# A fused retention and MoE kernel on one core: paired attention blocks and DMA transposes from unit 8 on, in place of unit-by-unit heads and TensorE transposes up to unit 11

## The chip, the cores and the metric

The kernel runs on 1 core of one Trainium2 chip. The metric is the device time of one execution in microseconds (us); lower is better. All comparisons below use runs that the harness calls fast. The kernel before has two close levels, most runs at 313.1 to 313.9 us with a granted TensorE clock of 0.997 to 1.0, and some at 314.5 to 316.1 us with 0.989 to 0.995; both count as fast, so a difference under about 1% needs many runs here.

Engines are named as in the profile: PE is TensorE (PEld its weight loads), DVE VectorE, ACT ScalarE, POOL GpSimd (it issues the loads), SP SyncE (it issues outputs and DMA transposes).

## The reference

```python
# q, k, v: (8 batches, 8 heads, 576, 64) float32; w_in (512, 2048), w_out (2048, 512)
scores = (q @ k^T) / sqrt(64)                       # per batch and head
ret    = scores * Dmat                              # Dmat[i,j] = gamma_h ** (i-j) for i >= j, else 0
attn   = ret @ v
x = attn.transpose(0, 2, 1, 3).reshape(4608, 512)
h = x @ w_in
out = (h * sigmoid(1.702 * h)) @ w_out              # (4608, 512)
```

## The kernel before

The 4608 rows are cut into 36 *units* of 128 rows; four units make a *chunk* of 512 rows. For each unit the attention part needs k and q with the head dimension on the partitions (`qkT`). A unit then takes: `scores` (8 small matmuls from qkT, masked by DVE into `pm`), `inter` (from the running state `kv`), `values` (from `pm` and the scaled v, `vp`), `values_out` (into `xT`), and `state` (updates kv from k and vp). `up` and `up_half` multiply a chunk by w_in, ACT applies the gelu; `down` multiplies by w_out, 16 steps per chunk, each of 4 matmuls of 512 columns. Attention work is slipped between these steps so that PE never waits.

qkT is made in one of two ways:

```python
def transpose_pe(u, bank, eng):           # 8 matmuls against the identity, then one DVE copy
    for j in range(2 * HP):
        op("pe", matmul(t[:, j, :], kq[sl][:, j // HP, ...], ident, is_transpose=True), ...)
    op("dve", tensor_copy(qkT[u % NQT], t), reads=[bank], writes=[f"qkT{u % NQT}"])

def transpose_dma(u):                     # one DMA, SBUF to SBUF, issued by SP
    op("sp", dma_start_transpose(qkT[u % NQT], kq[sl]),
       reads=[f"kq{sl}_0", f"kq{sl}_1"], writes=[f"qkT{u % NQT}"], dma=f"d_qkT{u % NQT}")
```

Before, units 0 to 11 are transposed on PE and units 12 to 35 by DMA. The order of loads on POOL, and the part of the program that the change touches (cut):

```python
for u in range(4, 8): load_kq(u); load_v(u)
for i in range(4):    load_wout(i)
for u in (8, 9):      load_kq(u); load_v(u)
# ... heads of units 0-3, chunk 0 up ...                      (units 10, 11 loaded here; then fetch(6))
play(8, lambda i: up_half(1, i, 1), {
    2: [lambda: head_in(8, "dve")],      # head_in = transpose_pe
    4: [lambda: head_mid(8)],            # head_mid = scores, scale v, mask
    6: [lambda: head_out(8)],            # head_out = inter, values, values_out, state
    7: [lambda: head_in(9, "dve")],
})
ready_t(6)                               # DMA transposes of units 12, 13
fetch(7, [f"qkT{13 % NQT}"])             # loads of 14, 15, held until unit 13's transpose has landed
play(16, lambda i: down(0, i, ("H0", "H1")), {
    1: [lambda: head_mid(9)],
    3: [lambda: head_in(10, "dve"), lambda: head_out(9)],
    # ... 10 and 11 in the same way, ready_t(7), fetch(8, held) ...
})
# from here on: block(m) handles units 2m and 2m+1 together, between down and up steps
```

`play(n, step, events)` runs step 0 to n-1 and the listed events after the numbered step.

Of the kernel before, what the change touches and what calls it, by code (L numbers as in the profile page):

```python
# [11 lines left out]
B, H, S, DH = 8, 8, 576, 64  # L12
# [3 lines left out]
NU = (B * S) // P  # L16
# [124 lines left out]
def bass_retnet_parallel__then__act_gelu_quick_kernel(  # L141
# [13 lines left out]
    with es:  # L155
# [40 lines left out]
        def load_kq(u, after=()):  # L196
            sl = u % NLD
            rows = unit_rows(u)
            for i, src in enumerate((k, q)):
                def f(e, src=src, i=i):  # L200
                    return [
                        e.dma_start(  # L202
                            kq[sl][p0 : p0 + n, i, :].rearrange("p (h d) -> p h d", d=DH),
                            src[b, :, s0 : s0 + n, :].rearrange("h p d -> p h d"),
                        )
                        for p0, n, b, s0 in rows
                    ]
                op("pool", f, reads=after, writes=[f"kq{sl}_{i}"], dma=f"d_kq{sl}_{i}", ndma=len(rows))

        def load_v(u, eng="pool"):  # L210
            sl = u % NVN
            rows = unit_rows(u)

            def f(e):
                return [
                    e.dma_start(  # L216
                        vn[sl][p0 : p0 + n, :, :],
                        v[b, :, s0 : s0 + n, :].rearrange("h p d -> p h d"),
                    )
                    for p0, n, b, s0 in rows  # L220
                ]
            op(eng, f, writes=[f"vn{sl}"], dma=f"d_vn{sl}_{eng}", ndma=len(rows))
# [147 lines left out]
        def inter(u):  # L370
            pb, kind, c = unit_info(u)
            qt = qkT[u % NQT]
            if c == 0:
                return
            bank = f"O{u % 2}"
            ob = by_pair(bank)
            for hp in range(HP):
                if kind < 2:
                    op("pe", lambda e, hp=hp: e.matmul(  # L379
                        ob[:, hp, :], kv[kind][c - 1][:, hp, :], qt[:, HP + hp, :],  # L380
                        start=(hp == 0), stop=True, skip_group_check=True),
                       reads=[f"kv{kind}_{c - 1}_0", f"kv{kind}_{c - 1}_1", f"qkT{u % NQT}"],
                       writes=[bank])
                else:
                    for b in range(2):
                        op("pe", lambda e, hp=hp, b=b: e.matmul(  # L386
                            ob[:, hp, 64 * b : 64 * b + 64], kv[b][3][:, hp, :],
                            qt[:, HP + hp, 64 * b : 64 * b + 64],
                            start=(hp == 0 and b == 0), stop=True, skip_group_check=True),
                           reads=[f"kv{b}_3_0", f"kv{b}_3_1", f"qkT{u % NQT}"], writes=[bank])  # L390
# [12 lines left out]
        def scores_out(u, hh, sb0=None):  # L403
            sb0 = 2 * (u % 2) if sb0 is None else sb0
            m = maskc if unit_info(u)[1] == 2 else mask
            bank = f"S{sb0 + hh}"
            op("dve", lambda e: e.tensor_tensor(  # L407
                pm[u % 4][hh].ap(), by_pair(bank), m[:, None, :].to_broadcast([P, HP, P]), ALU.mult),
               reads=[bank, "maskc" if m is maskc else "mask"], writes=[f"pm{u % 4}_{hh}"])

        def values(u):
            c = unit_info(u)[2]
            bank = f"O{u % 2}"
            ob = by_pair(bank)
            for hp in range(HP):
                for hh in range(2):
                    op("pe", lambda e, hp=hp, hh=hh: e.matmul(  # L417
                        ob[64 * hh : 64 * hh + 64, hp, :], vp[u % NVP][:, 2 * hp + hh, :],
                        pm[u % 4][hh][:, hp, :],
                        start=(c == 0 and hp == 0), stop=True, skip_group_check=True),  # L420
                       reads=[f"vp{u % NVP}", f"pm{u % 4}_{hh}"], writes=[bank])

        def values_out(u):
            ch, j = divmod(u, 4)
            ty = unit_info(u)[2]
            bank = f"O{u % 2}"
            op("dve", lambda e: e.tensor_tensor(  # L427
                xT[ch % 3][:, :, 128 * j : 128 * j + 128], by_pair(bank), gq[:, ty, :, :], ALU.mult),
               reads=[bank] + [f"gq{i}_{ty}" for i in range(HP)], writes=[f"xT{ch % 3}_{j}"])
# [65 lines left out]
        def head_in(u, eng, bank="S2"):  # L495
            transpose_pe(u, bank, eng)

        def head_mid(u):
            scores(u, 0)
            if u > 1:  # L500
                scale_v(u)
            scores_out(u, 0, 0)
            scores_out(u, 1, 0)

        def head_out(u, eng="dve"):
            inter(u)
            values(u)
            values_out(u)
            if u < 8:
                state_in_psum(u, "S3", eng)  # L510
            else:
                state(u, "S3")

        def fetch(m, after=()):
            for u in (2 * m, 2 * m + 1):
                if u < NU:
                    load_kq(u, after)
                    load_v(u)

        def ready_t(m):  # L520
            for u in (2 * m, 2 * m + 1):
                if u < NU:
                    transpose_dma(u)

        def ready_v(m):
            for u in (2 * m, 2 * m + 1):
                if u < NU:
                    scale_v(u)

        def block(m, done=False):  # L530

            a, b = 2 * m, 2 * m + 1
            nxt = 2 * m + 2 < NU
            if not done:
                inter(a)
                inter(b)
            if nxt:
                scores(a + 2)
                scores(b + 2)
                scores_out(a + 2, 0)  # L540
            if not done:
                values(a)
                values(b)
                values_out(a)
                values_out(b)
            if nxt:
                scores_out(a + 2, 1)
                scores_out(b + 2, 0)
                scores_out(b + 2, 1)
            fetch(m + 4)  # L550
            ready_t(m + 3)
            ready_v(m + 2)

        def states(m, i):
            u = 2 * m + (i == 4)
# [21 lines left out]
        for u in range(4, 8):  # L577
            load_kq(u)
            load_v(u)
        for i in range(4):  # L580
            load_wout(i)
        for u in (8, 9):
            load_kq(u)
            load_v(u)

        def play(n, step, events):
            for i in range(n):
                step(i)
                for f in events.get(i, ()):
                    f()  # L590
# [20 lines left out]
        warm(4)  # L611
        head_out(3, "act")
        setup_tail()
        for u in (10, 11):
            load_kq(u)
            load_v(u)
        warm(2)
        play(16, lambda f: up(0, f), {
            9: [lambda: head_in(4, "dve")],
# [3 lines left out]
            14: [lambda: head_mid(5)],  # L623
            15: [lambda: head_in(6, "dve"), lambda: head_out(5)],
        })
        fetch(6)
        head_mid(6)
        head_in(7, "dve")
        warm(1)
        play(8, lambda i: up_half(1, i, 0), {  # L630
            1: [lambda: head_out(6)],
            3: [lambda: head_mid(7)],
            5: [lambda: head_out(7)],
        })
        play(8, lambda i: up_half(1, i, 1), {
            2: [lambda: head_in(8, "dve")],
            4: [lambda: head_mid(8)],
            6: [lambda: head_out(8)],
            7: [lambda: head_in(9, "dve")],
        })  # L640
        ready_t(6)
        fetch(7, [f"qkT{13 % NQT}"])
        play(16, lambda i: down(0, i, ("H0", "H1")), {
            1: [lambda: head_mid(9)],
            3: [lambda: head_in(10, "dve"), lambda: head_out(9)],
            5: [lambda: head_mid(10)],
            7: [lambda: head_in(11, "dve"), lambda: head_out(10), lambda: ready_t(7), lambda: fetch(8, [f"qkT{15 % NQT}"])],
            9: [lambda: head_mid(11), lambda: ready_v(6)],
            11: [lambda: head_out(11)],
        })  # L650
        late = None
        for m in range(5, NU // 2 + 1):
            if m < NU // 2:
                block(m, m == 5)
            if late is not None:
                up(*late)
            c, h = divmod(m - 1, 2)
            iu = idn = 0
            for x in "UUDDUDUDUDUDDDUU" if m == 5 else "DDUDUDUDUDUDDUUU":
                if x == "D":  # L660
                    down(c - 1, 8 * h + idn, YB)
                    idn += 1
                else:
                    late = (c, 8 * h + iu)
                    if iu < 7:
                        up(*late)
                    iu += 1
                    states(m + 1, iu - 1)
# [62 lines left out]
```

## Time and profile before

| | before |
|---|---|
| time, median (range) of 6 runs taken with the change | 314.38 us (313.29 to 315.83) |
| PE busy | 303.9 us, 98% of the span |
| chain that ended last | PE 93% |
| DMA transposes | 24, median 12.4 us from issue to landing |

From the page of the kernel before: busy time of the engines; then PE and its granted clock in tenths over 40 slices of the span; then the engines' shares of the chain that ended last.

```profile
PE 303.9 (98%) x2174; PEld 156.4 (50%) x2174; DVE 134.3 (43%) x269; ACT 123.4 (40%) x222; POOL 106.5 (34%) x133
PE   8799999999999999999999999999999999999994
PEclk9999999999999999999999999999999999999999
PE 93%; POOL 3%; DMA 2%; DVE 1%; ACT 0%; issue 0%; POOLq 0%
```

PE is the bound, and it is not only "busy": the timeline shows matmuls of 512 columns starting 216 ns apart, without gaps. Busy time by 10 us stretches of the kernel before (columns: PE, PEld, DVE, ACT, POOL busy us with instruction counts, granted clock, DMA share, GB/s; packets overlap in the records, so a DMA share can be above 1):

```profile
50.00:60.00 10.00, 10.00 (x111) 7.65 (x110) 4.58 (x8) 4.58 (x8) 1.82 (x3) 1.00 1.79 175
60.00:70.00 10.00, 10.00 (x92) 5.36 (x90) 8.48 (x17) 1.19 (x2) 1.99 (x3) 1.00 1.19 173
70.00:80.00 10.00, 10.00 (x82) 5.04 (x77) 8.37 (x16) 2.39 (x4) 3.29 (x4) 1.00 1.44 185
80.00:90.00 10.00, 10.00 (x51) 4.63 (x49) 2.60 (x7) 3.38 (x6) 9.60 (x13) 1.00 1.27 132
```

A transpose on PE, in the timeline of the kernel before (start us, duration us, engine, line, what), is the second line here:

```profile
59.88 1.90 PE L469 MATMUL psH<-w_out_sb,gT 128*128 128x512 bf16 x8
61.62 0.61 PE L310 MATMUL psS<-ident,kq 128*128 128x128 bf16 x8
```

The next PE work starts 0.54 us after it (0.45 us for three of the four units). So four units cost PE 1.9 us. That is the most that removing these transposes can return directly.

A DMA transpose is another matter. The two lines are from the view of DMA issues of the kernel before, the first for the whole span (median us to landing), the second for 62 to 85 us, when fewer loads are queued:

```profile
qkT<-kq SPq DMA_TRANSPOSE x24, 12.4
qkT<-kq SPq DMA_TRANSPOSE x4, 3.7
```

The same instruction lands after 3.7 us or after 12.4 us, according to what else is queued.

### The profile page before, as it was taken

What the parts mean: (1) busy time and instruction counts of PE and PEld (TensorE: products, weight loads), DVE (VectorE), ACT (ScalarE), POOL (GpSimd) and SP (SyncE); (2) the same over time, 40 slices, a digit from 0 to 9 for tenths busy, and PEclk for the clock granted to TensorE, in tenths of its full rate; (3) what the DMA queues carried; (4) which work ended last, traced back from release to release, by engine and by line L of the source; (5) the groups of instructions that cost most, each with busy time, mean ns of one, the idle gap of its engine ahead of it and who ended that gap; (6) DMA issues with size and microseconds to landing.
All of it is one profiled execution on the core that took longest, in us unless ns stands there. A gap on an engine that the chain in (4) does not pass through costs nothing.

```text
span 311.3 us, 5152 instructions
## 1 busy us (share of the span) xinstructions
PE 303.9 (98%) x2174; PEld 156.4 (50%) x2174; DVE 134.3 (43%) x269; ACT 123.4 (40%) x222; POOL 106.5 (34%) x133
## 2 busy tenths in 40 slices
PE   8799999999999999999999999999999999999994
PEld 3444588655454545454545454545454545444442
DVE  4671884597445542546263625262627150100000
ACT  9676345201433333333333333333343434343411
POOL 9999933024699836154132323000000000000000
PEclk9999999999999999999999999999999999999999
DMA  9999999999999999999999999999910102010112
GB/s 133 184 206 187 190 200 184 175 172 165 173 120 207 139 141 167 141 147 159 116 150 113 153 91 173 113 175 110 161 67 2 68 2 67 2 67 34 36 67 67
DMA packets 114711, 39.14 MB, mean 126 GB/s; under 512 B 103808, under 2 KB 107904, under 8 KB 114688
## 3 DMA queue, kind: packets, MB, share of 16 engines
q0 software_dynamic: 82016, 22.55, 84.5%
q1 hardware_dynamic: 32672, 16.26, 35.8%
q8 instruction: 17, 0.28, 0.4%
q14 instruction: 6, 0.05, 0.1%
HBM read 36.70 MB, written 9.44 MB: 148 GB/s over the span
## 4 chain that ended last, share of the span: by engine, by line
PE 93%; POOL 3%; DMA 2%; DVE 1%; ACT 0%; issue 0%; POOLq 0%
PE psH L438 35%; PE psS L469 33%; PE psH L455 5%; PE psH L469 5%; PE psO L417 4%; PE psS L398 3%; PE psS L331 2%; PE psO L469 2%; POOL kq L202 2%; PE psO L379 2%; DMA kq<-in_q_dram 2%; PE psS L310 1%; PE psH L491 1%; PE psO L386 0%; POOL vn L216 0%; ACT kv_1 L344 0%
## 5 line engine op out<-in xcount | busy, mean ns | idle before, releaser
L438 PE MATMUL psH<-xT,w_in_sb 128*128 128x512 bf16 x512 | 127.3, 379 | 0.0
L443 ACT ACTIVATE gT<-psH 128x512 bf16<-128x512 f32 x128 | 76.5, 597 | 115.7 <-PE psH L438 115.7
L469 PE MATMUL psS<-w_out_sb,gT 128*128 128x512 bf16 x480 | 117.3, 379 | 0.0
L438 PEld LDWEIGHTS psH<-xT,w_in_sb 128*128 128x128 bf16 x512 | 47.8, 98 | 58.7 <-ACT gT L443 3.2
L469 PEld LDWEIGHTS psS<-w_out_sb,gT 128*128 128x128 bf16 x480 | 46.1, 98 | 51.7
L202 POOL DMA_DIRECT2D kq<-in_k_dram x40 | 37.4, 943 | 53.9 <-DMA qkT<-kq 22.4
L202 POOL DMA_DIRECT2D kq<-in_q_dram x40 | 36.8, 928 | 19.2 <-issue 19.0
L407 DVE TENSOR_TENSOR pm_0<-psS,mask 128x512 bf16<-128x512 f32 x32 | 22.0, 688 | 39.4 <-PE psS L398 39.3
L216 POOL DMA_DIRECT2D vn<-in_v_dram x38 | 35.6, 949 | 9.6 <-issue 5.1
L477 ACT ACTIVATE osb<-psS 128x512 f32<-128x512 f32 x30 | 17.9, 597 | 30.4 <-PE psS L469 30.4
L427 DVE TENSOR_TENSOR xT<-psO,gq 128x512 bf16<-128x512 f32 x36 | 23.6, 683 | 11.7 <-PE psO L417 11.7
L301 DVE TENSOR_TENSOR vp<-vn,vfac 128x512 bf16<-128x512 f32 x36 | 23.7, 685 | 1.3 <-DMA vn<-in_v_dram 1.1
L407 DVE TENSOR_TENSOR pm_1<-psS,mask 128x512 bf16<-128x512 f32 x32 | 21.8, 681 | 0.0
L361 DVE TENSOR_TENSOR kvf<-psS,kvf 64x256 f32<-64x256 f32 x24 | 10.1, 421 | 26.7 <-PE psS L331 26.5
L455 PE MATMUL psH<-xT,w_in_sb 128*128 128x256 bf16 x128 | 15.2, 273 | 0.0
L469 PE MATMUL psH<-w_out_sb,gT 128*128 128x512 bf16 x64 | 15.0, 380 | 0.0
L460 ACT ACTIVATE gT<-psH 128x512 bf16<-128x512 f32 x16 | 9.6, 598 | 11.5 <-PE psH L455 11.5
L455 PEld LDWEIGHTS psH<-xT,w_in_sb 128*128 128x128 bf16 x128 | 12.0, 98 | 1.9 <-issue 0.2
L417 PE MATMUL psO<-pm_0,vp 128*64 128x128 bf16 x144 | 12.9, 223 | 0.0
L359 DVE COPY kvf<-psS 64x256 f32<-64x256 f32 x12 | 5.1, 421 | 18.2 <-PE psS L331 18.1
L417 PE MATMUL psO<-pm_1,vp 128*64 128x128 bf16 x144 | 12.5, 223 | 0.3 <-DVE pm_1 L407 0.3
L317 DVE COPY qkT<-psS 128x1024 bf16<-128x1024 bf16 x9 | 6.2, 690 | 14.7 <-PE psS L310 14.6
(74 smaller groups left out, 179.9 us busy)
## 6 DMA issues: line engine op xcount, KB each, us to landing
out_dram<-osb SPq DMA_DIRECT2D x32, 256.0 KB, 5.7
vn<-in_v_dram POOLq DMA_DIRECT2D x30, 256.0 KB, 21.2
kq<-in_k_dram POOLq DMA_DIRECT2D x32, 128.0 KB, 18.6
kq<-in_q_dram POOLq DMA_DIRECT2D x32, 128.0 KB, 21.0
w_in_sb<-in_moe_w_in_dram POOLq DMA_DIRECT2D x4, 512.0 KB, 9.9
w_out_sb<-in_moe_w_out_dram POOLq DMA_DIRECT2D x4, 512.0 KB, 18.9
vn<-in_v_dram POOLq DMA_DIRECT2D x8, 128.0 KB, 25.6
out_dram<-osb SPq DMA_DIRECT2D x8, 128.0 KB, 5.7
```

The source lines that it names most:

```text
L202: e.dma_start(kq[sl][p0 : p0 + n, i, :].rearrange("p (h d) -> p h d", d=DH), src[b, :, s0 : s0 + n, :].rearrange("h p d -> p h d"),)
L216: e.dma_start(vn[sl][p0 : p0 + n, :, :], v[b, :, s0 : s0 + n, :].rearrange("h p d -> p h d"),)
L301: op("dve", lambda e: e.tensor_tensor(vp[u % NVP].ap(), vn[sl].ap(), vfac[:, ty, :, None].to_broadcast([P, H, DH]), ALU.mult), reads=[f"vn ...
L361: op("dve", lambda e, d=acc, s=src: e.tensor_tensor(d, s, d, ALU.add), reads=[bank, kfk], writes=[kfk])
L407: op("dve", lambda e: e.tensor_tensor(pm[u % 4][hh].ap(), by_pair(bank), m[:, None, :].to_broadcast([P, HP, P]), ALU.mult), reads=[bank, " ...
L417: op("pe", lambda e, hp=hp, hh=hh: e.matmul(ob[64 * hh : 64 * hh + 64, hp, :], vp[u % NVP][:, 2 * hp + hh, :], pm[u % 4][hh][:, hp, :], st ...
L427: op("dve", lambda e: e.tensor_tensor(xT[ch % 3][:, :, 128 * j : 128 * j + 128], by_pair(bank), gq[:, ty, :, :], ALU.mult), reads=[bank] + ...
L438: op("pe", lambda e, a=a: e.matmul(hb, w_in_sb[:, a, P * f : P * f + P], xT[c % 3][:, a, :], start=(a == 0), stop=(a == HP - 1)), reads=[f ...
L443: op("act", lambda e: e.activation(gT[c % 2][:, f, :], hb, AF.Gelu_apprx_sigmoid), reads=[bank], writes=[f"gT{c % 2}_{f}"])
L455: op("pe", lambda e, a=a, f=f, j=j: e.matmul(hb[:, j, :], w_in_sb[:, a, P * f : P * f + P], xT[c % 3][:, a, n], start=(a == 0), stop=(a == ...
L469: op("pe", lambda e, f=f: e.matmul(y, gT[c % 2][:, f, P * r : P * r + P], w_out_sb[:, f, :], start=(f == 0), stop=(f == NF - 1)), reads=[f ...
L477: op("act", lambda e: e.activation(osb[o].ap(), y, AF.Copy), reads=[bank], writes=[f"osb{o}"])
```

## The change

Its intent: free PE of the transposes of units 8 to 11, and handle units 8 to 11 in pairs as the later ones are. To have qkT of 8 and 9 in time, their k and q are loaded before w_out. The core of the diff (signatures, comments and the `done` argument of `block` cut):

```diff
         for u in range(4, 8):
             load_kq(u)
             load_v(u)
+        load_kq(8)
+        load_kq(9)
         for i in range(4):
             load_wout(i)
-        for u in (8, 9):
-            load_kq(u)
-            load_v(u)
+        load_v(8)
+        load_v(9)
+        load_kq(10)
+        load_kq(11)
...
-            5: [lambda: head_out(7)],
+            5: [lambda: head_out(7), lambda: ready_t(4)],
         })
+        for u in (12, 13):
+            load_kq(u)
+        for u in (12, 13, 14, 15):
+            load_v(u)
         play(8, lambda i: up_half(1, i, 1), {
-            2: [lambda: head_in(8, "dve")],
-            4: [lambda: head_mid(8)],
-            6: [lambda: head_out(8)],
-            7: [lambda: head_in(9, "dve")],
+            5: [lambda: scores_of(4), lambda: ready_v(4)],
         })
-        ready_t(6)
-        fetch(7, [f"qkT{13 % NQT}"])
+        ready_t(5)
         play(16, lambda i: down(0, i, ("H0", "H1")), {
-            1: [lambda: head_mid(9)],
-            3: [lambda: head_in(10, "dve"), lambda: head_out(9)],
...
+            1: [lambda: state(9)],
+            5: [lambda: ready_v(5)],
+            8: [lambda: block(4), lambda: ready_t(6), lambda: fetch_kq(7, 13), lambda: fetch_v(8)],
+            11: [lambda: state(10)],
+            13: [lambda: state(11)],
+            15: [lambda: ready_t(7), lambda: fetch_kq(8, 15), lambda: ready_v(6)],
         })
...
-            for x in "UUDDUDUDUDUDDDUU" if m == 5 else "DDUDUDUDUDUDDUUU":
+            for x in "DDDDBDDUDDUUUUUUU" if m == 5 else "DDUDUDUDUDUDDUUU":
+                if x == "B":
+                    block(m)
+                    continue
```

`ready_t(m)` issues the DMA transposes of units 2m and 2m+1, `scores_of(4)` computes the scores of units 8 and 9, and `block(4)` finishes 8 and 9 and computes the scores of 10 and 11.

More of the change, by code (lines that the diff above doesn't have):

```diff
@@ L512, in head_out, with fetch_kq, fetch_v @@
                 state(u, "S3")
-        def fetch(m, after=()):
+        def fetch_kq(m, held=None):
             for u in (2 * m, 2 * m + 1):
                 if u < NU:
-                    load_kq(u, after)
+                    load_kq(u, () if held is None else [f"qkT{held % NQT}"])
+        def fetch_v(m):
+            for u in (2 * m, 2 * m + 1):
+                if u < NU:
                     load_v(u)
@@ L528, in ready_v, with scores_of, block @@
                     scale_v(u)
-        def block(m, done=False):
+        def scores_of(m):
+            for u in (2 * m, 2 * m + 1):
+                scores(u)
+            for u in (2 * m, 2 * m + 1):
+                scores_out(u, 0)
+                scores_out(u, 1)
+        def block(m):
             a, b = 2 * m, 2 * m + 1
             nxt = 2 * m + 2 < NU
-            if not done:
-                inter(a)
-                inter(b)
+            inter(a)
+            inter(b)
             if nxt:
@@ L540, in block @@
                 scores_out(a + 2, 0)
-            if not done:
-                values(a)
-                values(b)
-                values_out(a)
-                values_out(b)
+            values(a)
+            values(b)
+            values_out(a)
+            values_out(b)
             if nxt:
@@ L549, in block @@
                 scores_out(b + 2, 1)
-            fetch(m + 4)
-            ready_t(m + 3)
-            ready_v(m + 2)
+            if m > 4:
+                fetch_kq(m + 4)
+                fetch_v(m + 4)
+                ready_t(m + 3)
+                ready_v(m + 2)
         def states(m, i):
@@ L613, in bass_retnet_parallel__then__act_gelu_quick_kernel @@
         setup_tail()
-        for u in (10, 11):
-            load_kq(u)
-            load_v(u)
+        load_v(10)
+        load_v(11)
         warm(2)
@@ L625, in bass_retnet_parallel__then__act_gelu_quick_kernel @@
         })
-        fetch(6)
         head_mid(6)
@@ L632, in bass_retnet_parallel__then__act_gelu_quick_kernel @@
             3: [lambda: head_mid(7)],
-            5: [lambda: head_out(7)],
+            5: [lambda: head_out(7), lambda: ready_t(4)],
         })
+        for u in (12, 13):
+            load_kq(u)
+        for u in (12, 13, 14, 15):
+            load_v(u)
         play(8, lambda i: up_half(1, i, 1), {
-            2: [lambda: head_in(8, "dve")],
-            4: [lambda: head_mid(8)],
-            6: [lambda: head_out(8)],
-            7: [lambda: head_in(9, "dve")],
-        })
-        ready_t(6)
-        fetch(7, [f"qkT{13 % NQT}"])
+            5: [lambda: scores_of(4), lambda: ready_v(4)],
+        })
+        ready_t(5)
         play(16, lambda i: down(0, i, ("H0", "H1")), {
-            1: [lambda: head_mid(9)],
-            3: [lambda: head_in(10, "dve"), lambda: head_out(9)],
-            5: [lambda: head_mid(10)],
-            7: [lambda: head_in(11, "dve"), lambda: head_out(10), lambda: ready_t(7), lambda: fetch(8, [f"qkT{15 % NQT}"])],
-            9: [lambda: head_mid(11), lambda: ready_v(6)],
-            11: [lambda: head_out(11)],
+            1: [lambda: state(9)],
[4 more added lines that the diff above has]
+            15: [lambda: ready_t(7), lambda: fetch_kq(8, 15), lambda: ready_v(6)],
         })
@@ L652, in bass_retnet_parallel__then__act_gelu_quick_kernel @@
         for m in range(5, NU // 2 + 1):
-            if m < NU // 2:
-                block(m, m == 5)
+            if 5 < m < NU // 2:
+                block(m)
             if late is not None:
@@ L658, in bass_retnet_parallel__then__act_gelu_quick_kernel @@
             iu = idn = 0
-            for x in "UUDDUDUDUDUDDDUU" if m == 5 else "DDUDUDUDUDUDDUUU":
+            for x in "DDDDBDDUDDUUUUUUU" if m == 5 else "DDUDUDUDUDUDDUUU":
+                if x == "B":
+                    block(m)
+                    continue
                 if x == "D":
-                    down(c - 1, 8 * h + idn, YB)
+                    down(c - 1, 8 * h + idn, ("S2", "S0") if m == 5 else YB)
                     idn += 1
```

## The prediction

> **What bounds the kernel now.** TensorE. In the busy time by 10 us stretches PE is 10.00 of 10.00 from 40 to 300 us; in the chain of waits PE holds 93% of the span. In the timeline matmuls start back to back, 216 ns each at 512 columns. DMA is the second limit: until 222 us it is seldom idle, and in the steady state the DMA transposes into qkT land only 5 to 10 us before PE uses them (DMA issues with landing times against the timeline: units 18/19 landed at 116.9, used at 121.6 us).
>
> **What the change removes.** PE transposes of units 8 to 11: 0.45 to 0.54 us per unit in the timeline, 1.9 us on the critical path. Scores of two units together save a little (16 matmuls in 0.55 us, against 2 x 0.33), as do fewer switches inside the down steps (0.09 us each). Together an estimated 2 to 2.8 us. Four DVE copies of 0.69 us go too, off the path.
>
> **What it adds.** Four DMA transposes, put where the load queue is full. Alone, a transpose lands 3.1 to 4.6 us after its issue (those issued from 62 to 77 us). With loads queued beside it this is 9 to 13 us (from 85 us on); two together took 13.9 us (85.55 to 99.41). The packet records: from 110 to 117.5 us the queues advanced alike, 1180 load and 1185 transpose-queue packets, about 100 ns per pair on each of 16 engines, though a load packet alone needs 20 ns and a transpose packet 23. The Trainium skill, "DMA: Bandwidth & Descriptors", Queues, rings and completion order, says that each engine round-robins between queues at packet granularity; the equal counts agree. The slowdown is the trace's.
>
> **How it should run (estimates from those numbers).** Loads of units 8 and 9 land at about 39.7 and 41.4 us; their transposes alternate with w_out packets (77 ns alone), and unit 9's lands at 54 to 64 us. PE wants it at 54, after the sixth half-up step: stall 0 to 10 us, middle 4. k and q of unit 10 land at 56 us plus the two transposes' cost, about 62; the transposes of 10 and 11 share the engines with queued loads and land 14 us later, 73 to 80. PE unstalled reaches block(4) at 64 us. So both stalls together should be 9 to 16 us. Units 12/13 may add 0 to 4 us at block(5). Such stalls may also halve the matmul rate afterwards (the Trainium skill, "TensorE: Matmul & The Clock Gate", Part 1; here the first warm-up matmuls show 412 ns against 216): 0 to 3 us. From block(7) on DMA catches up, and the rest should look as before, only later.
>
> **Prediction.** 325 us, range 311 to 335. Faster by over 2%: 0.03; within 2%: 0.25; slower: 0.72.
>
> **Right or wrong.** Right if PE has gaps before the scores of units 8/9 (near 54 us) and 10/11 (64 to 80 us), released by the DMA that writes qkT; the four new transposes take 8 to 20 us to land; w_out lands past 52 us (48 before); from 130 us on PE is as busy as before. Each gap's length proves its term.
>
> **What would make it wrong.** If transposes beside w_out's larger packets don't slow the queue, unit 9 lands by 54 us, kq 10/11 at 60, and the stall is a few us; if all four also land in 4 us, there is no stall, and the result is 310.5 us. If the backlog is not made good, the loss exceeds 20 us.

## The result, and the profile after

327.34 us median (324.36 to 328.15, 6 runs) against 314.38 us; ratio 1.0394, 95% interval 1.0339 to 1.0448: slower. Ratios in this document are the mean time of one kernel's fast runs over that of the other's fast runs of the same rounds, so they are not quite the ratio of the medians.

The same parts of the page as before, now of the changed kernel:

```profile
PE 306.9 (94%) x2142; PEld 157.0 (48%) x2142; DVE 132.6 (41%) x265; ACT 123.4 (38%) x222; POOL 106.7 (33%) x133
PE   7799998592999999999999999999999999999995
PEclk9899999596799999999999999999999999999999
PE 75%; DMA 15%; POOL 8%; SPq 0%; ACT 0%; issue 0%; POOLq 0%
```

The chain now runs for 15% of the span through DMA. The PE slices have two holes, and below them the granted clock falls. The stretches of the changed kernel:

```profile
50.00:60.00 10.00, 6.40 (x63) 4.93 (x60) 1.41 (x3) 4.64 (x8) 1.76 (x2) 0.93 1.54 141
60.00:70.00 10.00, 9.26 (x50) 5.25 (x51) 5.18 (x10) 1.79 (x3) 0.00 (x0) 0.73 1.85 158
70.00:80.00 10.00, 3.84 (x33) 1.94 (x33) 0.71 (x2) 0.60 (x1) 0.00 (x0) 0.78 1.33 201
80.00:90.00 10.00, 10.00 (x60) 4.81 (x61) 6.08 (x13) 0.60 (x1) 5.80 (x7) 0.70 0.91 106
145.00:245.00 100.00, 100.00 (x689) 50.09 (x687) 44.87 (x91) 38.09 (x64) 18.37 (x22) 1.00 1.07 128
```

Apart from a slower head, which the account below names, all damage lies between 50 and 90 us; from 145 to 245 us PE is as full as ever (last line). In 80 to 90 us PE counts as fully busy at a clock of 0.70: busy time alone would have hidden that loss. The holes by name, from the timeline of the changed kernel (in brackets: idle time before, and what ended it):

```profile
56.84 0.40 PE L398 MATMUL psS<-qkT 64*128 64x128 bf16 x8 [0.83 <-DMA qkT<-kq]
60.74 0.61 PE L398 MATMUL psS<-qkT 64*128 64x128 bf16 x8 [3.51 <-DMA qkT<-kq]
61.28 3.60 PE L455 MATMUL psH<-xT,w_in_sb 128*128 128x256 bf16 x16
...
73.38 0.40 PE L398 MATMUL psS<-qkT 64*128 64x128 bf16 x8
79.94 0.61 PE L398 MATMUL psS<-qkT 64*128 64x128 bf16 x8 [6.16 <-DMA qkT<-kq]
81.47 4.95 PE L469 MATMUL psH<-w_out_sb,gT 128*128 128x512 bf16 x12
```

PE waits 0.83 us for the transpose of unit 8, 3.51 us for that of unit 9 and 6.16 us for that of unit 11, 10.5 us in all. After each long wait the next matmuls are slow. Measured from start to start, the 16 half-up matmuls at 61.28 took 3.39 us (1.76 at full rate), and the 12 down matmuls at 81.47 took 4.78 us (2.60). With two smaller pieces (0.30 and 0.43 us) the low rate cost 4.5 us. The account of the two profiled runs: 326.4 - 311.3 = 15.1 us, of which 10.5 are waits, 4.5 the low rate, 1.9 a slower head (PE reached the first up step at 21.9 instead of 20.0 us, in code that the change doesn't touch: its granted clock was 0.5 from 14.2 to 17.7 us; the trace of pe_8_9 below has the same dip, the others have none, so I put it down to chance), less a saving of about 1.9 us, which is what remains and was not measured by itself. Whether the slower level of the kernel before is the same dip, no trace shows.

The transposes and loads themselves. This list is drawn from the trace's DMA issues and the semaphore updates of their landing (us):

```
                         before          changed kernel
                         landed          issued   landed   took
w_out, last quarter       48.0                     57.4
v of unit 9               54.2                     59.3
k, q of unit 11           59.0                     63.6
k, q of unit 13           64.4                     76.7
transpose of unit 8      (on PE)         41.4     56.8     15.4
transpose of unit 9      (on PE)         42.8     60.7     17.9
transpose of unit 10     (on PE)         61.9     71.0      9.0
transpose of unit 11     (on PE)         63.7     79.9     16.2
```

From 45 to 57.5 us the packet records (counted by their ends, semaphore writes included) show 1872 packets of the load queue and 1787 of the transposes' queue: one to one, 109 ns per pair on each of the 16 engines (16 x 12500 / 1830).

### The profile page after: what moved, and what is told of

The parts are those of the page before. It is cut to its first block, busy times and chain, and to the rows that moved or that the text cites. A ratio compares the mean times of both kernels' runs of the same rounds, so it can differ in the third digit from the quotient of the medians.

```text
span 326.4 us, 5092 instructions
## 1 busy us (share of the span) xinstructions
PE 306.9 (94%) x2142; PEld 157.0 (48%) x2142; DVE 132.6 (41%) x265; ACT 123.4 (38%) x222; POOL 106.7 (33%) x133
## 4 chain that ended last, share of the span: by engine, by line
PE 75%; DMA 15%; POOL 8%; SPq 0%; ACT 0%; issue 0%; POOLq 0%
PE psS L469 32%; PE psH L438 30%; DMA qkT<-kq 10%; POOL kq L202 5%; DMA kq<-in_q_dram 5%; PE psO L417 3%; PE psH L469 3%; PE psS L398 2%; PE psO L469 2%; POOL vn L216 2%; PE psS L331 2%; PE psO L379 1%; POOL w_in_sb L225 1%; PE psH L455 1%; SPq L322 0%; PE psO L386 0%
## 5 line engine op out<-in xcount | busy, mean ns | idle before, releaser
L216 POOL DMA_DIRECT2D vn<-in_v_dram x38 | 34.2, 927 | 21.7 <-issue 21.7
L407 DVE TENSOR_TENSOR pm_0<-psS,mask 128x512 bf16<-128x512 f32 x32 | 22.0, 688 | 43.7 <-PE psS L398 43.5
L427 DVE TENSOR_TENSOR xT<-psO,gq 128x512 bf16<-128x512 f32 x36 | 23.4, 683 | 17.7 <-PE psO L417 17.7
L301 DVE TENSOR_TENSOR vp<-vn,vfac 128x512 bf16<-128x512 f32 x36 | 23.5, 685 | 1.3 <-DMA vn<-in_v_dram 1.2
L398 PE MATMUL psS<-qkT 64*128 64x128 bf16 x288 | 12.9, 225 | 10.5 <-DMA qkT<-kq 10.5
L407 DVE TENSOR_TENSOR pm_1<-psS,mask 128x512 bf16<-128x512 f32 x32 | 21.8, 681 | 0.0
L469 PE MATMUL psH<-w_out_sb,gT 128*128 128x512 bf16 x64 | 17.2, 427 | 0.0
L455 PE MATMUL psH<-xT,w_in_sb 128*128 128x256 bf16 x128 | 16.6, 291 | 0.0
L398 PEld LDWEIGHTS psS<-qkT 64*128 64x128 bf16 x288 | 8.5, 97 | 15.1 <-DMA qkT<-kq 11.1
```

The source lines that it names most:

```text
L216: e.dma_start(vn[sl][p0 : p0 + n, :, :], v[b, :, s0 : s0 + n, :].rearrange("h p d -> p h d"),)
L301: op("dve", lambda e: e.tensor_tensor(vp[u % NVP].ap(), vn[sl].ap(), vfac[:, ty, :, None].to_broadcast([P, H, DH]), ALU.mult), reads=[f"vn ...
L398: op("pe", lambda e, hp=hp, hh=hh, bank=bank: e.matmul(by_pair(bank)[:, hp, :], qt[64 * hh : 64 * hh + 64, hp, :], qt[64 * hh : 64 * hh + ...
L407: op("dve", lambda e: e.tensor_tensor(pm[u % 4][hh].ap(), by_pair(bank), m[:, None, :].to_broadcast([P, HP, P]), ALU.mult), reads=[bank, " ...
L427: op("dve", lambda e: e.tensor_tensor(xT[ch % 3][:, :, 128 * j : 128 * j + 128], by_pair(bank), gq[:, ty, :, :], ALU.mult), reads=[bank] + ...
L455: op("pe", lambda e, a=a, f=f, j=j: e.matmul(hb[:, j, :], w_in_sb[:, a, P * f : P * f + P], xT[c % 3][:, a, n], start=(a == 0), stop=(a == ...
```

## The experiments

Each is an edit of the changed kernel, or of another experiment where it says so, and each is correct against the reference. The theory that I went in with: **a DMA transpose that shares the engines with queued loads becomes slow and slows the loads too; PE then waits for qkT, and its clock falls.** Rivals: the paired blocks or the new load order cost the time; loads are late whatever the transposes do; the clock dips for another reason.

### 1. All transposes up to unit 11 back on PE (pe_all)

```diff
-            5: [lambda: head_out(7), lambda: ready_t(4)],
+            5: [lambda: head_out(7)],
...
+            1: [lambda: head_in(8, "dve")],
+            3: [lambda: head_in(9, "dve")],
             5: [lambda: scores_of(4), lambda: ready_v(4)],
...
-        ready_t(5)
...
-            5: [lambda: ready_v(5)],
+            3: [lambda: head_in(10, "dve")],
+            5: [lambda: head_in(11, "dve"), lambda: ready_v(5)],
```

> The changed kernel with units 8 to 11 transposed on TensorE again; pairing, load order and moved blocks stay. Theory (the four transposes by DMA among queued loads are what is late): both stalls go, 312 to 315 us, ratio to the kernel before 0.995 to 1.005. Rival (the load order or the paired blocks cost the time): it stays above 320 us. PE waits for qkT by DMA: near 0 before 85 us.

Measured: 312.66 us (312.51 to 314.05, 4 runs), ratio 0.9975 (0.9944 to 1.0006). The whole loss is gone, while load order, pairing and moved blocks are still there. That rival falls. Repeated with more rounds:

> pe_all once more, with more rounds: whether pairing the blocks alone, with every transpose up to unit 11 on TensorE, beats the kernel before. The timeline gives it about 0.6 us fewer switches and paired scores: ratio 0.996 to 0.999, 312.2 to 313 us.

Measured: 312.54 us (6 runs), ratio 0.998 (0.9954 to 1.0006). Twice the same size, 0.2%, twice just short of clear of 1. In the profiled runs the span is 310.7 and 310.6 us against 311.3.

### 2. Half of it on PE (pe_10_11 and pe_8_9)

pe_10_11 takes only the last two hunks of pe_all; pe_8_9 only the first two.

> Units 8 and 9 by DMA as in the changed kernel, 10 and 11 on TensorE. Theory: the first stall (3.9 us before the scores of unit 9) and its 2 us at half rate stay, the second goes except for k and q of unit 11 landing at about 63.6 us; 317 to 321 us. Rival, that only the order of loads matters: as the changed kernel, 327.

Measured: 318.31 us (317.95 to 319.36), ratio 1.0151 (1.0117 to 1.0186). The time is as expected; the stall was 5.1 us instead of 3.9.

> Units 8 and 9 on TensorE, 10 and 11 by DMA. Theory: no stall near 54 us, but PE reaches block(4) at about 65 us and the transposes of 10 and 11, issued at 56 to 58 us, share the engines with queued loads and land 13 to 14 us later, near 71: a stall of 5 to 7 us, and 2 us more at half rate; 318 to 322 us.

Measured: 329.59 us (327.51 to 330.25), ratio 1.0494 (1.0452 to 1.0536): the first stall is gone as expected, but the second is more than twice what I expected, and the whole is slower than with all four by DMA. The wait lines of pe_10_11 and then of pe_8_9 (us in total, times, longest):

```profile
PE psS L398 <- DMA qkT<-kq: 5.1, 1, 5.1
```

```profile
PE psS L398 <- DMA qkT<-kq: 14.4, 2, 8.6
```

In pe_8_9 the transposes of 10 and 11 were issued at 57.3 and 59.0 us, earlier than in the changed kernel, and landed at 76.2 and 82.6 us, later. The sign of the theory holds, but my 14 us for a pair was no constant: this pair took 25 us. Alternation of packets cannot be the reason, because from 67.5 to 77.5 us the load queue moved only 198 packets, and the transposes' queue still no more than 1191, 119 per us; with the loads held (next experiment) it moves 700 per us. What else is there shows when each DMA is split into its 16 parts. The records have 16 raises of its semaphore for every DMA, which I take as one for each part; these are their times, in order (us):

```
pe_8_9, q of unit 13        62.5 62.5 62.5 62.6 62.6 62.6 62.6 63.5 65.6 66.4 66.4 68.1 69.0 71.7 75.9 78.4
pe_8_9, transpose of 10     74.2 75.0 75.0 75.2 75.4 75.5 75.5 75.5 75.5 75.5 75.5 75.5 75.5 75.5 75.5 76.2
pe_8_9, transpose of 11     82.4 82.4 82.4 82.4 82.5 82.5 82.5 82.5 82.5 82.5 82.5 82.5 82.5 82.5 82.5 82.6
held_to_13, transpose of 10 57.8 57.8 57.8 57.9 57.9 57.9 57.9 57.9 57.9 57.9 58.0 58.0 58.0 58.0 58.0 58.0
```

The parts of a load end up to 16 us apart: some parts are through all queued loads early (in pe_8_9 seven parts of the last queued load are in by 68.7 us), others are far behind. The parts of a transpose end together, and late. This fits a transpose whose parts advance in step, so that it goes at the pace of the engine that is furthest behind; then a few lagging engines hold it for long, though the others have nothing else to do. The last experiment, 7, tests this.

### 3. Hold the loads while a transpose runs (gated)

```diff
         load_kq(9)
+        ready_t(4)
         for i in range(4):
-            load_wout(i)
+            load_wout(i, ["qkT9"] if i == 0 else ())    # POOL waits for unit 9's transpose
...
-        load_v(10)
+        ready_t(5)
+        load_v(10, "pool", ["qkT1"])                     # POOL waits for unit 11's (slot 1)
```

> All four by DMA as in the changed kernel, but the loads behind them are held: w_out until unit 9's transpose has landed, v of unit 10 and what follows until unit 11's has. Theory (sharing the engines with loads makes a transpose slow): each of the four lands within 3 to 6 us of its issue, unit 9's by 47 us, unit 11's by 69, although w_out lands no earlier (57 to 58 us) and k and q of 11 land at about 63; first stall 0 to 1 us, second about 3; 314 to 318 us. Rival (a transpose takes 9 to 18 us there whatever else is queued, or the loads as such are late): 323 us or more.

Measured: 326.0 us, median of the three fast runs (323.31 to 327.54; a fourth, slow one took 329.63), ratio 1.0378 (1.0311 to 1.0445). My time was wrong, but the mechanism showed as it should. With nothing beside them the four transposes landed 5.1, 4.5, 3.2 and 3.1 us after issue, and PE waited 1.0 us for qkT. It waited for something else instead (waits of gated):

```profile
PE psS L331 <- DVE vp L301: 6.9, 1, 6.9
PE psS L331 <- DVE pm L407: 1.9, 1, 1.9
PE psS L398 <- DMA qkT<-kq: 1.0, 1, 1.0
```

L331 is `state`, which needs the scaled v. Holding w_out emptied the load queue: k and q of unit 9 landed at 41.2 us, and the first quarter of w_out only at 52.3 us. w_out was complete at 62.0 us (expected 57 to 58) and v of unit 9 landed at 64.6 us, while PE wanted it at 58. The delay changed its name and hardly its length. So the transposes can be made fast, but the loads behind them pay.

### 4. The same transposes, read by nobody (shadow)

On top of pe_all, the four DMA transposes at the same places, into spare tiles:

```diff
+        spare = [sb(f"spare{i}", [P, 2 * HP, P], BF16) for i in range(4)]
+        def shadow(m): ...   # as transpose_dma, but into spare[u - 8]
-            5: [lambda: head_out(7)],
+            5: [lambda: head_out(7), lambda: shadow(4)],
+        shadow(5)
         play(16, lambda i: down(0, i, ("H0", "H1")), {
```

> pe_all (units 8 to 11 transposed on TensorE) with the changed kernel's four DMA transposes issued at the same places into spare tiles that nothing reads: same load on the queues, but PE waits for no transpose. If the loss is only PE waiting for the four transposes, time stays as pe_all, 312.7 us. If their queue load also delays the loads themselves, PE waits for v of unit 9 (vp, then the state matmuls, 59 us against 55) and for k and q of unit 11 (63.6 against 58.5): I expect 2 to 4 us of such waits, 314.5 to 318 us. Rival (the delay of loads is the whole loss): 322 us or more.

Measured: 321.46 us (319.3 to 322.13), ratio 1.0222 (1.0177 to 1.0267): 8.8 us above pe_all, though PE reads none of the four. I expected 2 to 5. The shadow transposes took 13 to 18 us each (9 to 18 in the changed kernel), and k and q of unit 13 landed at 78.5 us instead of 64.5 in pe_all. I had followed the delay only to unit 11; it travelled on to the transposes of 12 and 13, which landed at 84.5 and 85.4 us instead of 71.2 and 72.4. The wait of shadow, on those:

```profile
PE psS L407 <- DMA qkT<-kq: 5.0, 2, 4.5
```

After that wait the granted clock was 0.5 until 91.6 us, so the low rate is part of the 8.8 us too. More than half of the loss (8.8 of 14.7 us between the medians of pe_all and the changed kernel; by the ratios, which compare runs of the same rounds, 7.7 of 13.1 us) comes with the load that four transposes put on the queues, whoever reads them. The two shares do not simply add: with the readers there, PE is late itself and no longer meets the delay of 12 and 13.

### 5. Keep PE busy during the stalls (filled)

```diff
                 scores(u)                 # in scores_of
+                if u == 8:
+                    warm(16)              # 16 matmuls on zeros into a free bank
...
                 scores(a + 2)             # in block
+                if m == 4:
+                    warm(28)
```

> The changed kernel with 16 and 28 matmuls on zeros put where PE stalls (between the scores of units 8 and 9, and of 10 and 11), 3.5 and 6.1 us, about the lengths of the two stalls. Theory: the half rate after the stalls (3.39 us against 1.76 for the two half-up steps, 4.78 against 2.6 for twelve down matmuls) comes from PE being idle, so with PE kept busy the granted clock stays near 1 and 3.5 to 5 us come back: 322 to 324 us. Rival (the clock dips for another reason): 327 us.

Measured: 323.18 us (321.4 to 325.36), ratio 1.0303 (1.0256 to 1.0349): by the medians 4.2 us less than the changed kernel. The two ran in different rounds, though, and the two ratios leave only 2.9 us, with intervals that just overlap; between the profiled runs it is 4.6 us, of which 1.7 are the head's chance dip. The stretches of filled:

```profile
60.00:70.00 10.00, 10.00 (x64) 5.44 (x65) 5.29 (x10) 2.39 (x4) 0.00 (x0) 1.00 1.83 168
80.00:90.00 10.00, 10.00 (x71) 5.10 (x71) 6.17 (x15) 1.79 (x3) 4.15 (x5) 1.00 0.81 117
```

The granted clock stays at 1.00 where it was 0.73 and 0.70, although PE can still not go on before the same transposes have landed (beside the matmuls on zeros it waits 2.5 us for them). So the low rate was the price of idleness. It was a quarter to a third of the loss: 2.9 us by the ratios, 4.5 us in the changed kernel's trace.

### 6. Can DMA transposes pay here at all? (held_10_11, held_to_13, held_states)

held_10_11 keeps units 8 and 9 on PE, loads k and q of 10 and 11 before v of 8 and 9, and holds all later loads until unit 10's transpose has landed:

```diff
-        load_v(8)
-        load_v(9)
         load_kq(10)
         load_kq(11)
...
+        ready_t(5)
+        load_v(8, "pool", ["qkT0"])
+        for u in (9, 10, 11):
+            load_v(u)
...
+            5: [lambda: ready_v(4)],
+            6: [lambda: state(9)],
```

> pe_8_9 with k and q of units 10 and 11 loaded before v of 8 and 9, and every load after them held until unit 10's transpose has landed; state(9) and the v scalings moved later to fit. Theory: transposes of 10 and 11 land within 3 to 6 us of their issue, near 57 to 60 us, before block(4) at 66; v of 9 lands near 62 us, in time for state(9) after down step 6; units 12/13 near 76 us, block(5) at 78. No stall over 1 us; 311 to 313 us, ratio 0.990 to 0.997. If DMA falls behind instead, block(5) waits for unit 13 and it takes 314 to 318 us.

Measured: 314.7 us, median of the four fast runs (312.83 to 315.72; two slow ones took 317.73 and 319.85), ratio 1.0022 (0.9982 to 1.0063). The transposes landed at 57.8 and 59.6 us, 3.7 and 3.1 us after issue: as expected. But those of 12 and 13 then met four v loads and landed at 81.5 and 82.1 us, and PE waited for them: the outcome that I had named for the case that DMA falls behind, at its edge. (Its profiled run was a slow one; only landings and waits are read from it.) held_to_13 holds those v loads too:

```diff
-        for u in (12, 13, 14, 15):
-            load_v(u)
...
-  block(4), ready_v(5), ready_t(6), fetch_kq(7, 13), fetch_v(8)
+  block(4), ready_v(5), ready_t(6), load_v(12, held by unit 12's transpose), load_v(13),
+  fetch_kq(7, 13), fetch_v(7), fetch_v(8)
```

> held_10_11, with v of units 12 to 15 also held until unit 12's transpose has landed, and k and q of 14 and 15 moved ahead of v of 14 and 15. In held_10_11 the transposes of 12 and 13 shared the engines with four v loads and took 13 and 12 us, to 82 us, and PE waited for them. Theory: they now land within 3 to 6 us, by about 75 us, before block(5) at 78.6; unit 15's lands near 89 us, about when block(6) needs it: waits for qkT under 1.5 us; 311 to 313 us, ratio 0.991 to 0.998. If the hold only passes the delay on to units 14 and 15, 314 to 316 us as in held_10_11.

Measured: 313.87 us (313.51 to 315.4), ratio 1.0019 (0.9997 to 1.0041). No wait of PE for qkT is left. Four transposes between 35 and 80 us, from issue to landing (min/median/max): first the changed kernel's six, then the four of held_to_13:

```profile
DMA to landing us min/median/max: 6.0/12.3/17.9
```

```profile
DMA to landing us min/median/max: 3.1/3.2/3.7
```

But v is late by as much as k and q are early (waits of held_to_13):

```profile
PE psS L331 <- DVE vp L301: 2.0, 2, 1.1
```

held_states moves `state(9)` one and `state(10)`, `state(11)` two down steps later, past that wait:

> held_to_13 with the state matmuls of unit 9 one down step later and those of 10 and 11 two later: in held_to_13 PE waited 1.1 and 0.9 us there for scaled v, and for nothing else that is new. If these 2.0 us are all that it lost against its saved transposes, 311 to 312.5 us, ratio 0.993 to 0.998; rival (what is left is hidden elsewhere): as held_to_13, 1.000 to 1.003.

Measured: 314.49 us (312.99 to 316.43), ratio 1.0021 (0.9981 to 1.0061). My expectation failed, the rival was right. The wait moved again (held_states):

```profile
PE psS L469 <- DVE pm L407: 2.0, 1, 2.0
```

Now a down step waits for the masking of scores. The scaling of v of units 12 and 13 (`ready_v(6)`, L301) comes before that masking (L407) on DVE, and the timeline of DVE in held_states shows that DVE stands at that scaling until v has landed:

```profile
77.74 0.69 DVE L301 TENSOR_TENSOR vp<-vn,vfac 128x512 bf16<-128x512 f32 x1 [2.00 <-DMA vn<-in_v_dram]
79.52 0.69 DVE L301 TENSOR_TENSOR vp<-vn,vfac 128x512 bf16<-128x512 f32 x1 [1.09 <-DMA vn<-in_v_dram]
80.25 0.69 DVE L407 TENSOR_TENSOR pm<-psS,mask 128x512 bf16<-128x512 f32 x1
```

So it is v again that is late. Whether a later scaling would free the time, no run tried.

### 7. A few engines kept busy beside a transpose (burden)

On top of held_to_13, 24 loads of two rows of 8 KB each, read by nobody, behind k and q of unit 11 on the load queue. The result stays correct; only the landing of unit 10's transpose is of interest.

```diff
         load_kq(11)
+        for j in range(24):               # extra: a spare tile, two partitions each
+            op("pool", dma_start(extra[2 * j : 2 * j + 2, :], q[j % B] as [8, 36864] [0:2, 0:2048]), ...)
```

> held_to_13 plus 24 loads of two rows of 8 KB each, queued right behind k and q of unit 11, that nothing reads: they should keep a few of the 16 DMA engines busy for some us while the transpose of unit 10 runs. If a transpose's 16 parts advance in step with the furthest engine, all 16 of its semaphore raises come late and within 2 us of each other (58.0 us in held_to_13; 60 us or later here). If each part goes its own way, most of the 16 come at 58 us as before and only a few are late. If the extra loads spread over all 16 engines, the run tells nothing. The time itself doesn't matter.

Measured, in one look: 321.21 us, state unknown (a single run). Unit 10's transpose was issued at 54.95 us, and its 16 raises came from 62.6 to 63.6 us: all late, within 1.0 us. The packet records by us from the span's start (data packets of the two queues; an 8 KB packet took 309 ns):

```
us     8 KB load packets   transpose packets
56            6                  338
57            6                  115
58            6                    3
59            6                   74
60            3                  158
61            0                  744
62            0                  615
```

Six packets of 309 ns in a us are the time of about two engines of the 16. With no more than that beside it, the transpose fell to 88 packets per us on average from 57 to 61 us, and once the last of them was through it ran at full rate. The extra loads were meant to sit on a few fixed engines. Which ones they took, the records don't tell, but the starts of their 48 packets form two chains, 311 to 314 ns from one start to the next until 59.1 us: two engines with room for little else. Until 58.0 us the transpose moved 454 packets (from this an estimate: some 30 for each of the other 14 engines), and then 2 in the next us. From 59.3 to 61.0 us it came in bursts of 20 to 40 packets, one every 0.31 to 0.34 us, which is the rhythm of the 8 KB packets (0.34 to 0.37 us there). So a transpose may run some packets ahead, but then goes at the pace of the engines that are held up most, not at that of the average engine. That is shown here, in one run; which step of the hardware ties the parts together is not.

### What the experiments leave

No version with DMA transposes for 8 to 11 beat pe_all, and pe_all itself is at 0.998 of the kernel before, with an interval that still touches 1.

## Why the prediction was right or wrong

The prediction (325 us, 311 to 335, slower) held; point by point:

- *Bound and saving.* PE was the bound. The saving of 2 to 2.8 us fits: the account above leaves 1.9 us, as a remainder.
- *Sharing.* Predicted about 100 ns per pair of packets; 109 ns beside w_out. Holding the loads (gated) brought the same transposes from 9 to 18 us down to 3 to 5. That queued loads make them slow is shown. But alternation was the wrong picture of it, or half of it: in pe_8_9 and burden transposes crawl beside very few load packets, because they go at the pace of the engines held up most. The pair of pe_8_9 took 25 us for that reason, against my 14.
- *Landings.* Unit 9's transpose predicted at 54 to 64 us, measured 60.7; k and q of 10 at about 62, measured 61.9; transposes of 10 and 11 at 73 to 80, measured 71.0 and 79.9.
- *Waits.* First stall predicted 0 to 10, middle 4: 4.3 us. Both together 9 to 16: 10.5 us. Units 12/13 0 to 4: none, since they landed at 82.7 and 83.5 us and block(5) came at 93.6.
- *Low rate.* Predicted 0 to 3 us, measured 4.5 in the trace and 2.9 (by the ratios) to 4.2 (by the medians) by filling the stalls. This term was too small in the prediction: after the first stall 1.9 us were lost, after the second 2.6.
- *Later stages.* As before, only later: PE 100.00 of 100 us from 145 to 245 us.
- *What I had not seen.* I treated the loss as a wait for four transposes. shadow shows that their load on the queues delays whatever PE needs next, even if nobody reads them; gated, held_to_13 and held_states show that holding the loads only hands the delay to v, and held_10_11 that it can go to the next transposes. In none of the orders tried here did the DMA engines have time for these transposes before 75 us without PE waiting for some other transfer.
- *Luck.* That 325 came so near to 327.34 us is in part luck. The waits and their cause were right, but the low rate was above its range and units 12/13 cost nothing, and the two errors offset each other; the 14 us for a pair was right for neither the second pair of the changed kernel (18 us from the first issue to the last landing) nor that of pe_8_9.

## What to carry to other kernels

Before moving work from a busy engine to DMA, look at what the queues hold at that moment: the same transpose landed in 3 us alone and in 9 to 24 us among loads, and it slowed the loads too; two engines' worth of other traffic cut its rate from over 600 packets per us to 88. A saving of 1.9 us on the bounding engine was worth less than the DMA time that it took, because each way of protecting the transposes made another transfer late. When an otherwise full PE gets a hole of several us, count the slow matmuls after it as well: after holes of 3.5 and 6.2 us they were 4.5 us here, on top of 10.5 us of waits; the hole of 2.0 us in held_states was followed by no drop of the clock.

## What the Trainium skill lacked or had wrong

- "DMA: Bandwidth & Descriptors", Queues, rings and completion order, says that each engine round-robins between queue rows by packets. The equal counts beside w_out agree (1872 and 1787). It does not say what it costs a DMA transpose: its packets advanced at 119 per us in pe_8_9 while the load queue moved only 20 per us, against 700 per us with the loads held, and its 16 parts ended within 2 us of each other where those of a load ended 16 us apart. In burden, six 8 KB packets per us, about two engines' time, brought it from over 600 packets per us to between 3 and 158 (88 on average). No page says that a transpose goes at the pace of its most delayed engine.
- The same page has, in its Rules for kernel authors, that "A transpose next to ordinary DMAs needs nothing". That is about correctness, and all results here were correct; for time it misleads: two transposes took 18.5 us (changed kernel) or 24.6 us (pe_8_9) from the first issue to the start of their 2048th packet beside loads, and 3.9 to 5.4 us where the loads were held (gated, held_to_13).
- No page has the wait before a transpose's first packet under load: 3.9 to 4.5 us after the issue where loads were queued (changed kernel, shadow, pe_8_9, pe_10_11), 1.2 to 1.3 us where they were held (gated, held_to_13). But it was 1.3 us too for unit 12 of the kernel before and unit 10 of burden, with loads still in the queue, so queued loads alone don't explain it. What it waits for is open.
- "TensorE: Matmul & The Clock Gate", Part 1, has the half rate after about 3.4 us of idleness; the stalls of 3.5 and 6.2 us agree, with most matmuls after them at 213 instead of 110 ns (256 columns) and 427 instead of 216 ns (512 columns). It does not say that matmuls on zeros are enough to keep the clock up; filled shows it, at 1.00 instead of 0.70.
